# Retention and an exact-GELU MLP on one core: another hand-planned order of groups, with ten chunks turned on TensorE and later places for v and the DMA turns

## The chip, the cores and the metric

The kernel runs on one core of a Trainium2 chip. The metric is the device time of one execution in microseconds. Eight runs of the kernel before have a median of 293.14 us (291.69 to 297.92).

## The reference

Batch 8, 8 heads, sequence 576, head dimension 64; the MLP takes 4608 tokens of width 512 through a hidden width of 2048.

```python
scores = scale * np.matmul(q, k.transpose(0, 1, 3, 2))
gamma = 1.0 - 2.0 ** (-5.0 - np.arange(H))
Dmat = np.where(rel >= 0, gamma[:, None, None] ** rel, 0.0)   # rel = row - column
ret = np.matmul(scores * Dmat, v)
x = ret.transpose(0, 2, 1, 3).reshape(B * S, H * D)
h = x @ w_in
out = (0.5 * h * (1.0 + erf(h / sqrt(2)))) @ w_out
```

All inputs and the output are float32; the kernel computes in bfloat16 with float32 accumulation.

## The kernel before

The sequence of each batch is cut into five chunks, four of 128 tokens and a short one of 64, so that there are 40 chunks. Within a chunk, attention is done with a masked product of scores; what came before a chunk enters through a running state. For a chunk the kernel does these steps:

- load q, k and v, cast to bfloat16, by three to five DMAs of POOL's queue (`load_chunk`, L232 and L236). Nine sets of buffers hold loaded chunks. The loads of w_in (L247, eight pieces) and w_out (L255, eight pieces) stand in the same queue, in the order that the string LOADS writes out ("i", "o" and chunk numbers);
- `turn`: transpose q and k into qkT. The first N_PE_TR chunks are turned on TensorE (L326, L328) and copied out of PSUM by DVE or ACT (L331, L334); the others are turned by a DMA that SP issues (L315). SP also issues the stores of the output (L662, L664);
- `scaled_v`: multiply v by its decay into vh, on DVE (L412);
- `together`: the scores of new chunks, and the products of the state with q of chunks pending (L362); `masked`: the causal mask, on DVE straight from PSUM or by an ACT copy first (L401, L403), as ACT_MASK and the planned load of both engines decide;
- `inner` (o_ps, L438) and `states` (u_ps, L460), whose sum run_sum DVE keeps (L469, L472, L478) and ACT copies out (L475);
- `evacuate`: DVE multiplies o_ps by its decay into xT (L490).

These come in groups: an entry of PLAN says how many new chunks a group takes (0, 1 or 2), how much MLP work is to lie before it, and whether the products ahead of the next group are cut into halves of 64 rows of output. The chunks taken by the last group are the pending ones of the next.

The MLP works on blocks of 512 tokens. The first product makes hT (L303) which ACT turns into g by a GELU (L532). The first N_DYN blocks may take their tokens in pieces, as they come ready. The second product, called fast, multiplies quarter matrices with seven products in place of eight; it needs sums of g, called s, made by DVE (L562 to L565), and sums of w_out, called w_sum (L546 to L549). From block 7 on (N_LEAN) the first product is done so too (lean).

The order is written by a planner that runs while the program is built. It holds a clock, the busy times of DVE and ACT, the eight PSUM banks and a model of the transfers, and at each step emits what is due: a group, a turn, a scaling of v, sums, or else a step of the MLP. Each engine then runs its own instructions in just this order, waiting where the real data is late. A scaling of v is offered when the model says that v has landed, and a turn by DMA when k has; a group when the masks, states, turns and banks that it needs are ready by the model. In the model a load takes LD_FIX + transfer + LD_TAIL, and a DMA turn T_FIX + T_DMA + T_TAIL:

```python
def load(took, at, key, issue=0.87):
    pool_at[0] = max(pool_at[0], clock[0]) + issue
    transfer(0, pool_at[0] - issue + LD_FIX, took, LD_TAIL, at, key)
...
i = nxt["V"]
if i < nxt["T"] and i < nxt["S"] + 5:
    got.append((land_v[i], "V", i))
```

Of the kernel before, what the change touches and what calls it, by code (L numbers as in the profile page):

```python
# [16 lines left out]
def kernel(  # L17
# [24 lines left out]
    C = 128  # L42
# [4 lines left out]
    NCH = -(-S // C)  # L47
    chunks = [(b, ci, ci * C, min(C, S - ci * C)) for b in range(B) for ci in range(NCH)]
    N_CH = len(chunks)
    N_PE_TR = 9  # L50
    N_FIRST = 4
    N_LD = 9
    N_RING = 4
    LD_FIX = 2.5
    LD_TAIL = 1.9
    T_FIX = 2.4
    T_TAIL = 4.2
    T_DMA = 1.8
    N_DYN = 2
    N_LEAN = 7  # L60
    LEAN_FIRST = 1
    LOADS = "1 2 3 i i i 4 5 6 i i i 7 i i 8 o o o o o o o o"
    T_LEAD = 5
    TR_LEAD = 5
    POOL_0 = 1.05
    LAND_0 = (2.9, 4.0, 3.9)
    COLS = ()
    CLOCK_0 = 3.2
    ACT_MASK = 0.3
    X_FROM = 10  # L70
    PLAN = [(1, 207, 1), (1, 571, 0), (0, 547, 0), (2, 777, 0), (1, 404, 0), (2, 522, 0), (1, 106, 0), (1, 13, 1), (2, 31, 0), (1, 74, 0), (0, 58, 0), (1, 9, 0), (2, 46, 0), (1, 68, 0), (2, 53, 0), (2, 58, 0), (2, 6, 0), (2, 102, 0), (2, 3, 1), (2, 116, 0), (2, 78, 0), (2, 78, 0), (2, 34, 0), (0, 6, 0), (2, 51, 1), (2, 51, 0), (2, 35, 1), (0, 0, 1)]
    FAST_FROM = 0
    HALF = TOK_BLK // 2
    COL = d_model // 2
# [23 lines left out]
    clock = [0.0]  # L98
# [12 lines left out]
    def on_dve(ready, n, rate=1):  # L111
        return on("DVE", ready, n / rate / 960 + 0.072)
# [17 lines left out]
    turned = const_pool.tile([128, 32], FP32, name="turned")  # L130
# [44 lines left out]
    land_in, land_out = [1e6] * (N_DF // 2), [None] * (N_DF // 2)  # L175
    w_sum = const_pool.tile([128, 4, N_DF // 2, COL], BF16, name="w_sum")
    land_q, land_k, land_v = {}, {}, {}
    rings = ([], [])
    dma_at = [0.0]
    pool_at = [POOL_0]  # L180
# [22 lines left out]
    def transfer(ring, start, took, tail, at, key):  # L203
# [4 lines left out]
        ahead = tuple([list(job) for job in q_] for q_ in rings)  # L208
        serve(ahead, dma_at[0], 1e5, True)

    def load(took, at, key, issue=0.87):
        pool_at[0] = max(pool_at[0], clock[0]) + issue
        transfer(0, pool_at[0] - issue + LD_FIX, took, LD_TAIL, at, key)

    def head_of(i, place):
# [3 lines left out]
    def load_chunk(i, now=0.0):  # L219
        b, ci, c0, cs = chunks[i]  # L220
        if i == 0:
            loaded[i] = (qk0, v0)
            transfer(1, LAND_0[1] - 3.0, 1.1, 1.0, land_k, i)
            transfer(0, LAND_0[2] - 1.7, 0.87, 0.9, land_v, i)
            land_q[i], land_k[i], land_v[i] = on_dve(LAND_0[0], 512, 1.5), on_dve(LAND_0[1], 512, 1.5), LAND_0[2]
            return
        qk = ld_pool.tile([128, 2, H, D], BF16, tag="qk", name="qk_ld")
        v_ld = ld_pool.tile([128, H, D], BF16, tag="v", name="v_ld")
        for dst, src, at_ in ((qk[:, 0], q, land_q), (qk[:, 1], k, land_k), (v_ld, v, land_v)):
            if i >= X_FROM and src is not v:  # L230
                for odd in range(2):
                    nc.gpsimd.dma_start(dst[:cs, HP * odd:HP * odd + HP],  # L232
                                        src[b, odd::2, c0:c0 + cs, :].rearrange("h s d -> s h d"))
                    load(0.435 * cs / C, at_, i, 0.73)
                continue
            nc.gpsimd.dma_start(dst[:cs], src[b, :, c0:c0 + cs, :].rearrange("h s d -> s h d"))  # L236
            load(0.87 * cs / C, at_, i)
        loaded[i] = (qk, v_ld)

    W_IN_COLS = 256  # L240
# [3 lines left out]
    def load_w_in():  # L244
        j = len(w_in_sb)
        t = const_pool.tile([128, N_DM, W_IN_COLS], BF16, name=f"w_in{j}")
        nc.gpsimd.dma_start(  # L247
            t, moe_w_in[:, j * W_IN_COLS:(j + 1) * W_IN_COLS].rearrange("(c p) f -> p c f", p=128)
        )
        w_in_sb.append(t)  # L250
        load(1.34, land_in, j)

    def load_w_out():
        j = next(j for j in range(N_DF) if land_out[j] is None)
        nc.gpsimd.dma_start(  # L255
            w_out_sb[:, j], moe_w_out[j * 256:(j + 1) * 256, :].rearrange("(c p) f -> p c f", p=128)
        )
        load(1.34, land_out, j)

    load_chunk(0)  # L260
    for what in LOADS.split():
        if what == "i":
# [6 lines left out]
    st = {i: {} for i in range(N_CH)}  # L269
# [35 lines left out]
    def turn(i, parts=(0, 1)):  # L305
# [7 lines left out]
        qkT = s["qkT"]  # L313
        if i >= N_PE_TR:
            nc.sync.dma_start(qkT.rearrange("p j hp s -> p (j hp) s")[:, :, :cs],  # L315
                              qk[:cs].rearrange("p j h d -> p (j h d)"), transpose=True)
            transfer(1, clock[0] + T_FIX, T_DMA * cs / C, T_TAIL, s, "turned")
            return
# [73 lines left out]
    def masked(i):  # L392
# [3 lines left out]
        for e in range(2):  # L396
            r = ret_short[e] if cs < C else ret_pool.tile([128, HP, 128], BF16, tag=f"ret{e}", name=f"ret{e}")
            on_both = max(busy["ACT"], ready) + 0.6 <= max(busy["DVE"], ready) + ACT_MASK
            src, begin = sc[e][:cs, :, :cs], ready
# [428 lines left out]
    stages = []  # L828
    first_runs = [[[("d", t, m)] for m in range(N_DF)] for t in range(N_DYN)]
    second_run = [[("s", t, n) for n in range(len(FAST_ORDER))] for t in range(N_BLK)]  # L830
    stages = [first_runs[0], first_runs[1] + [second_run[0]], [second_run[0]] + first_runs[1], [second_run[1]] + (first_runs[2] if N_DYN > 2 else [])]
    for t in range(2, N_BLK):
        if t < N_LEAN:
            stages.append([[("1", t, m, 0, TOK_BLK) for m in range(N_DF)]] if t >= N_DYN else first_runs[t])
        lean_runs = [[("f", t + 1, n, x) for x in range(len(FIRST_ORDER))] for n in range(N_DF // 4)]
# [49 lines left out]
    def state_to(pend, new):  # L885
        return max([-1] + pend[-1:] + ([new[-1] - 1] if new else []))
# [10 lines left out]
    def group_ready(pend, new):  # L897
        when = max([0.0] + [max(st[i]["masked"], st[i].get("scaled", 1e6)) for i in pend])
        for i in pend:
            if chunks[i][1] > 0:  # L900
                when = max(when, st[i].get("u_end", 0.0) - 0.5)
        when = max([when] + [st[i].get("turned", 1e6) - 0.3 * len(pend) for i in new])
        n = 2 if pend else 0
        for i in range(nxt["U"], state_to(pend, new) + 1):
            if chunks[i][1] + 1 < NCH:
                when = max(when, st[i].get("scaled", 1e6))
                n = 3 if pend else 1
        if n:
            when = max(when, banks_at(n))
        if new:  # L910
            when = max(when, banks_at(n + 2 * len(new)) - 0.3 * n)
        return when

    def attention_picks():
        got = []
        pend, i = held(), nxt["R"]
        pick = mlp_pick()
        kind, t = pick[1][0][:2] if pick is not None else ("s", N_BLK)
        starved = pick is None or pick[0] > clock[0] + 0.3

        if nxt["P"] < len(PLAN):
            size, due, _ = PLAN[nxt["P"]]
            new = list(range(i, i + size))
            if (paced[0] >= due or starved) and i + size <= nxt["T"]:
                got.append((group_ready(pend, new), "G", (pend, new)))
        i = nxt["V"]
        if i < nxt["T"] and i < nxt["S"] + 5:
            got.append((land_v[i], "V", i))
        i = nxt["T"]
        if i < N_CH and i in land_v and i <= nxt["S"] + (T_LEAD if i < N_PE_TR else TR_LEAD):  # L930
            if i >= N_PE_TR:
                got.append((land_k[i], "T", i))
            elif i >= N_FIRST:
                got.append((max(land_k[i] + 0.1, banks_at(2)), "T", i))
            else:
                got.append((max((land_q, land_k)[half[0]][i] + 0.1, banks_at(1)), "T", i))
        if to_sum and fast_done.get(to_sum[0][0] - 1, 0) >= 12:
            got.append((g_ready(to_sum[0][0], 0, TOK_BLK, range(4 * to_sum[0][1], 4 * to_sum[0][1] + 4)) - 0.1, "Z", 0))
        if gelus:
            got.append((gelus[0][0] - 0.1, "H", 0))  # L940
        j = len(w_in_sums)
        if N_LEAN < N_BLK and j < len(w_in_sb) and N_CH - 1 in loaded and nxt["S"] > N_CH - N_LD + j and nxt["U"] > N_CH - N_LD + j:
            got.append((busy["DVE"] + 0.1, "Y", j))
        t = N_LEAN + len(x_sums)
        if t < N_BLK and nxt["V"] == N_CH and x_ready(t * TOK_BLK, (t + 1) * TOK_BLK) < 1e5:
            got.append((max(busy["DVE"] + 0.1, x_ready(t * TOK_BLK, (t + 1) * TOK_BLK)), "X", t))
        if weights_due:
            got.append((weights_due[0][0], "W", 0))
        return got
# [6 lines left out]
    def attend(kind, i):  # L956
        if kind == "G":
            pend, new = i
            nxt["P"] += 1
            p = nxt["P"]  # L960
            by_col[0] = p < len(PLAN) and PLAN[p][2] > 0
            upto = state_to(pend, new)
# [130 lines left out]
```

## Time and profile before

| | |
|---|---|
| median of 8 runs | 293.14 us |
| profiled execution | 293.15 us, span 291.4 us |
| PE busy | 278.7 us (96%) |
| DVE busy | 210.9 us (72%) |
| ACT busy | 155.4 us (53%) |
| POOL busy | 147.4 us (51%), nearly all before 190 us |
| first hT product | 17.34 us |
| last matmul ends | 287.88 us |

A line of the profile names engine, line, operation, and output and inputs by the program's names. "Busy" of PE counts a matmul from start to modelled end; they are pipelined, so start to start is the measure of rate. [...] Line numbers are those of the kernel before; in the changed one, everything behind the model of loads stands up to nine lines further down.

### The profile page before, as it was taken

Reading aid. Unit: us, or ns where it says so; the run is one execution under the profiler, and the core shown is the slowest. Engines: PE = TensorE matmul, PEld = TensorE weight load, DVE = VectorE, ACT = ScalarE, POOL = GpSimd, SP = SyncE. Lnnn points to the kernel's source line nnn. Section 1 sums busy time; section 2 is a strip of 40 time slices with the busy share of each in tenths; the row PEclk is TensorE's granted clock in tenths of the full one; section 3 lists DMA queues with packets and bytes.
Section 4 is the critical chain, followed back from the end, with each engine's and each line's share of the span. In section 5 each row is a group of like instructions: output and inputs, shape, how many; then the busy total and the mean of one; then the engine's idle time right before and its main releaser. Section 6 shows DMA issues by size and latency. Waiting matters only on the chain.

```text
span 291.4 us, 8239 instructions
## 1 busy us (share of the span) xinstructions
PE 278.7 (96%) x3396; PEld 203.2 (70%) x3410; DVE 210.9 (72%) x530; ACT 155.4 (53%) x318; POOL 147.4 (51%) x198
## 2 busy tenths in 40 slices
PE   6799999999999699999999999989999999999995
PEld 2477565988864288557874687548854888888884
DVE  7679982769866974798388747799667885985552
ACT  3766667232356443675167724764257487587221
POOL 8998757997775996884995499200000000000000
PEclk9999999999999799999999999999999999999999
DMA  9999999999999999999999999970030000210123
GB/s 136 156 168 176 177 206 146 141 180 208 154 197 166 137 156 139 166 192 128 147 155 185 136 147 174 133 113 2 2 145 0 2 0 3 107 39 0 75 108 108
DMA packets 154565, 35.79 MB, mean 123 GB/s; under 512 B 143264, under 2 KB 150432, under 8 KB 154528
## 3 DMA queue, kind: packets, MB, share of 16 engines
q0 software_dynamic: 117792, 18.10, 94.8%
q1 hardware_dynamic: 36736, 17.18, 34.1%
q8 instruction: 26, 0.43, 0.7%
q14 instruction: 11, 0.09, 0.1%
HBM read 36.70 MB, written 9.44 MB: 158 GB/s over the span
## 4 chain that ended last, share of the span: by engine, by line
PE 46%; DMA 23%; POOL 16%; DVE 8%; issue 5%; ACT 0%; POOLq 0%; ACTq 0%; DVEq 0%
PE fast L303 24%; DMA v_ld<-in_v_dram 14%; PE hT L303 13%; POOL qk_ld L232 7%; PE lean L303 7%; DMA w_in<-in_moe_w_in_dram 5%; DMA w_out<-in_moe_w_out_dram 3%; POOL v_ld L236 3%; POOL qk_ld L236 3%; POOL w_in L247 1%; DVE s L563 1%; DVE s L562 1%; DVE s L565 1%; PE o_ps L438 1%; DVE ret L403 1%
## 5 line engine op out<-in xcount | busy, mean ns | idle before, releaser
L303 PE MATMUL hT<-xT,w_in 128*128 128x512 bf16 (+7 forms) x639 | 102.6, 341 | 3.8 <-DVE run_sum L472 3.0
L303 PEld LDWEIGHTS <-w_in 128*128 128x128 bf16 (+1 forms) x748 | 59.4, 101 | 50.8 <-DVE run_sum L472 4.0
L532 ACT ACTIVATE g<-hT 128x512 bf16<-128x512 f32 (+5 forms) x143 | 68.8, 507 | 32.5 <-PE hT L303 32.0
L303 PEld LDWEIGHTS <-s 128*128 128x128 bf16 x576 | 56.1, 98 | 6.9 <-DVE s L563 0.2
L232 POOL DMA_DIRECT2D qk_ld<-in_k_dram x60 | 44.1, 752 | 17.5 <-DMA v_ld<-in_v_dram 12.8
L303 PE MATMUL fast<-w_sum,s 128*128 128x256 bf16 x432 | 50.0, 273 | 0.0
L232 POOL DMA_DIRECT2D qk_ld<-in_q_dram x60 | 44.7, 766 | 6.8 <-PE hT L303 4.3
L303 PEld LDWEIGHTS <-g 128*128 128x128 bf16 (+1 forms) x456 | 41.8, 99 | 5.9 <-DVE u_sb L478 0.4
L236 POOL DMA_DIRECT2D v_ld<-in_v_dram x39 | 34.3, 879 | 7.9 <-DVE xT L490 2.8
L303 PE MATMUL fast<-w_out,g 128*128 128x256 bf16 (+1 forms) x312 | 33.8, 273 | 0.0
L654 DVE TENSOR_TENSOR o_sb<-fast,u 128x512 f32<-128x512 f32 (+1 forms) x20 | 12.7, 633 | 26.8 <-ACT u L650 16.2
L650 ACT COPY u<-fast 128x512 f32<-128x512 f32 (+1 forms) x20 | 10.9, 543 | 36.0 <-PE fast L303 36.0
L412 DVE TENSOR_TENSOR vh<-v_ld,dv 128x512 bf16<-128x512 bf16 x32 | 21.5, 680 | 7.5 <-DMA v_ld<-in_v_dram 7.5
L490 DVE TENSOR_TENSOR xT<-o_ps,dq 128x256 bf16<-128x256 f32 (+1 forms) x84 | 26.6, 374 | 0.0
L403 DVE TENSOR_TENSOR ret<-sc,msk 128x512 bf16<-128x512 f32 x29 | 19.1, 683 | 3.5 <-PE o_ps L362 2.8
L475 ACT CAST u_sb<-run_sum 128x256 bf16<-128x256 f32 x24 | 9.7, 405 | 20.5 <-DVE run_sum L469 11.0
L562 DVE TENSOR_TENSOR s<-g 128x512 bf16<-128x512 bf16 x36 | 15.0, 417 | 6.7 <-ACT g L532 6.2
L401 ACT CAST ret<-sc 128x512 bf16<-128x512 f32 x35 | 19.0, 585 | 0.4 <-PE o_ps L362 0.4
L303 PE MATMUL fast<-w_sum,g 128*128 128x256 bf16 x144 | 17.2, 273 | 0.0
L303 PE MATMUL fast<-w_out,s 128*128 128x256 bf16 x144 | 17.2, 272 | 0.0
L563 DVE TENSOR_TENSOR s<-s,g 128x512 bf16<-128x512 bf16 x36 | 15.3, 425 | 1.2
L362 PE MATMUL sc<-qkT 64*64 64x128 bf16 (+1 forms) x576 | 15.7, 220 | 0.1
(89 smaller groups left out, 338.1 us busy)
## 6 DMA issues: line engine op xcount, KB each, us to landing
out_dram<-o_sb SPq DMA_DIRECT2D x16, 512.0 KB, 6.0
v_ld<-in_v_dram POOLq DMA_DIRECT2D x32, 128.0 KB, 6.0
qk_ld<-in_q_dram POOLq DMA_DIRECT2D x50, 64.0 KB, 6.2
qk_ld<-in_k_dram POOLq DMA_DIRECT2D x50, 64.0 KB, 5.5
w_in<-in_moe_w_in_dram POOLq DMA_DIRECT2D x8, 256.0 KB, 6.8
w_out<-in_moe_w_out_dram POOLq DMA_DIRECT2D x8, 256.0 KB, 8.7
out_dram<-o_sb SPq DMA_DIRECT2D x8, 128.0 KB, 1.7
qk_ld<-in_q_dram POOLq DMA_DIRECT2D x7, 128.0 KB, 6.9
```

The costliest lines, as they stand in the source:

```text
L232: nc.gpsimd.dma_start(dst[:cs, HP * odd:HP * odd + HP], src[b, odd::2, c0:c0 + cs, :].rearrange("h s d -> s h d"))
L236: nc.gpsimd.dma_start(dst[:cs], src[b, :, c0:c0 + cs, :].rearrange("h s d -> s h d"))
L303: nc.tensor.matmul(out_[sl], lhsT=lhsT[:, sl], rhs=rhs, start=start, stop=stop, skip_group_check=True)
L362: nc.tensor.matmul(out_, lhsT=lhsT, rhs=rhs, start=start, stop=stop, skip_group_check=True)
L401: nc.scalar.copy(r[:cs, :, :cs], src)
L403: nc.vector.tensor_tensor(r[:cs, :, :cs], src, msk[:cs, :, :cs].to_broadcast([cs, HP, cs]), op=ALU.mult)
L412: nc.vector.tensor_tensor(vh[:cs], loaded[i][1][:cs], dv[:cs, :, ci:ci + 1].to_broadcast([cs, H, D]), op=ALU.mult)
L490: nc.vector.tensor_tensor(xT[:, g::2, at:at + hi - lo], s["o_ps"][g][:, s["place"], :, lo:hi], dq[:, g::2, c0 + lo:c0 + hi], op=ALU.mult)
L532: nc.scalar.activation(g_of(t, m, lo, hi), hT[:, :hi - lo], AF.Gelu)
L562: nc.vector.tensor_tensor(u[:, 0], a[2, 1], a[2, 2], op=ALU.add)
L563: nc.vector.tensor_tensor(u[:, 1], u[:, 0], a[1, 1], op=ALU.subtract)
L654: nc.vector.tensor_tensor(dst, psum(where), f[to][:, sl], op=ALU.add)
```

## The change

It gives the planner other constants and another PLAN, of 34 entries in place of 28. The model of loads lets a load begin only when the eighth load before it has landed. Chunk 9, a short one, is turned on TensorE too. For the chunks turned by DMA, the scaling of v is offered V_SAFE = 3 us after v has landed in the model, and a group that takes the chunk as new G_SAFE = 1.5 us after its turn. N_DYN goes from 2 to 4, and the mask takes the way over ACT less readily. The loads of w_in stand earlier among the chunks. No instruction's kind changes and nothing is added to the loop over chunks; what moves is the order on each engine, and how many pieces the MLP products are cut into.

```diff
-    N_PE_TR = 9
+    N_PE_TR = 10
...
-    LD_FIX = 2.5
-    LD_TAIL = 1.9
-    T_FIX = 2.4
-    T_TAIL = 4.2
-    T_DMA = 1.8
-    N_DYN = 2
+    LD_FIX = 2.0
+    LD_TAIL = 1.7
+    T_FIX = 2.1
+    T_TAIL = 2.6
+    T_DMA = 1.95
+    N_DYN = 4
...
-    LOADS = "1 2 3 i i i 4 5 6 i i i 7 i i 8 o o o o o o o o"
+    LOADS = "1 2 3 i i i i 4 5 i 6 i i 7 i 8 o o o o o o o o"
     T_LEAD = 5
-    TR_LEAD = 5
+    V_SAFE = 3
+    G_SAFE = 1.5
+    TR_LEAD = 6
...
-    ACT_MASK = 0.3
+    ACT_MASK = -0.5
...
-    PLAN = [(1, 207, 1), (1, 571, 0), (0, 547, 0), (2, 777, 0), (1, 404, 0), (2, 522, 0), (1, 106, 0), (1, 13, 1), (2, 31, 0), (1, 74, 0), (0, 58, 0), (1, 9, 0), (2, 46, 0), (1, 68, 0), (2, 53, 0), (2, 58, 0), (2, 6, 0), (2, 102, 0), (2, 3, 1), (2, 116, 0), (2, 78, 0), (2, 78, 0), (2, 34, 0), (0, 6, 0), (2, 51, 1), (2, 51, 0), (2, 35, 1), (0, 0, 1)]
+    PLAN = [(1, 220, 1), (1, 524, 0), (1, 208, 0), (1, 297, 1), (0, 273, 0), (1, 263, 0), (2, 34, 0), (0, 57, 0), (1, 1, 1), (1, 4, 1), (1, 8, 0), (1, 43, 0), (2, 31, 0), (2, 53, 0), (2, 75, 0), (1, 21, 0), (2, 58, 0), (0, 102, 0), (2, 38, 0), (0, 7, 1), (1, 75, 0), (0, 13, 0), (1, 46, 0), (0, 46, 0), (1, 25, 0), (2, 0, 0), (2, 122, 0), (2, 115, 0), (2, 92, 0), (2, 21, 0), (2, 65, 0), (2, 31, 1), (1, 78, 1), (0, 205, 1)]
...
     def load(took, at, key, issue=0.87):
-        pool_at[0] = max(pool_at[0], clock[0]) + issue
+        t = max(pool_at[0], clock[0])
+        if len(in_ring) >= 8:
+            a, k = in_ring[-8]
+            t = max(t, a[k])
+        in_ring.append((at, key))
+        pool_at[0] = t + issue
...
-        when = max([when] + [st[i].get("turned", 1e6) - 0.3 * len(pend) for i in new])
+        when = max([when] + [st[i].get("turned", 1e6) + (G_SAFE if i >= N_PE_TR else 0) - 0.3 * len(pend) for i in new])
...
-            got.append((land_v[i], "V", i))
+            got.append((land_v[i] + (V_SAFE if i >= N_PE_TR else 0), "V", i))
```

The model's transfer of a chunk's q, k or v goes from 0.87 to 0.93 (0.435 to 0.475 for the halves), of a piece of a weight from 1.34 to 1.25.

## The prediction

> **What bounds the kernel now.** I read the page first (engine shares, granted clock), then the waits by engine, then the timelines of DVE and PE around the long ones, then a table of windows, and last the instruction order of both versions.
>
> ```profile
> PE 278.7 (96%) x3396; PEld 203.2 (70%) x3410; DVE 210.9 (72%) x530; ACT 155.4 (53%) x318; POOL 147.4 (51%) x198
> ...
> PEclk9999999999999799999999999999999999999999
> ```
> TensorE is busy 96% of the span: it is the bound, and what moves the end is work added to it or idle time taken from it. One slice (the 14th) has a lower granted clock.
>
> ```profile
> DVE vh_short L412 <- DMA v_ld<-in_v_dram: 8.0, 3, 5.8
> DVE vh L412 <- DMA v_ld<-in_v_dram: 7.5, 7, 1.8
> ...
> PE hT L303 <- DVE run_sum L472: 3.0, 2, 2.2
> ```
> DVE stands 15.5 us in ten waits for a load of v. TensorE has two waits behind DVE's run_sum, 2.18 and 0.84 us. The timeline of DVE shows that they are one story:
>
> ```profile
> 94.40 0.68 DVE L412 TENSOR_TENSOR vh_short<-v_ld,dv 64x512 bf16<-64x512 bf16 x1 [1.66 <-DMA v_ld<-in_v_dram]
> ...
> 96.47 0.41 DVE L469 COPY run_sum<-u_ps 128x256 f32<-128x256 f32 x1
> 97.41 0.42 DVE L472 TENSOR_TENSOR run_sum<-run_sum,u_ps 128x256 f32<-128x256 f32 x1 [0.52 <-ACT u_sb L475]
> ```
> and the timeline of PE, where it ends:
> ```profile
> 97.88 2.61 PE L303 MATMUL hT<-xT,w_in 128*128 128x512 bf16 x8 [2.18 <-DVE run_sum L472]
> ```
> The columns are start, length, engine, line, operation, and in brackets the idle time before it. DVE runs in program order. Scaling the v of a short chunk (chunk 19) waits for its load until 94.40; behind it stand four sums of g and the run_sum copies, which alone free the PSUM bank of u_ps. The next hT has no bank until 97.8. At 188.34 the same happens with the v of chunk 38 (DVE waits 1.78, hT begins at 193.29 after 0.84).
>
> ```profile
> 95.70:98.00 2.30, 0.12 (x1) 0.11 (x2) 1.78 (x6) 0.54 (x2) 2.30 (x4) 1.00 2.56 141
> 98.00:104.00 6.00, 6.00 (x25) 2.73 (x24) 4.52 (x12) 4.02 (x8) 5.80 (x9) 0.72 1.96 134
> 192.00:194.00 2.00, 1.16 (x14) 0.40 (x10) 1.47 (x4) 1.13 (x3) 0.00 (x0) 1.00 0.73 134
> ```
> Columns: window, its length, busy of PE, PEld, DVE, ACT, POOL, then granted clock, DMA share, GB/s. After the 2.18 us of idleness the clock averages 0.72 for 6 us: 6 x 0.28 = 1.7 us lost on top. After 0.84 us it stays at 1.00. Apart from these, the first 17.34 us (until the first hT) and one gap of 0.32 at 256.7 before a lean product, PE has no idle stretch worth naming.
>
> **The change part by part.**
>
> Matmul work. From the two instruction orders: the hT products count 572 in full-width equivalents before (two 64-row halves are one) and 676 after, over the same columns; N_DYN = 4 cuts more blocks into pieces. 64 products of 64 columns took 1.87 us in the trace, 29.2 ns each against 26.7 for 64 columns[...], so 2.5 ns each: 104 x 2.5 = +0.3 us. More of fast and hT is cut into 64-row halves, which cost nothing: 24 halves of 512 columns (34.25 to 36.86) are 2.61 us, 0.2175 a pair, against 0.217 a whole. Chunk 9, a short one, is turned on TensorE: eight transposes, +0.33 (20.07 to 20.40). The attention stretches of PE go from 26 to 29. A stretch with one each of states, inner, scores, cross is 0.93 (75.94 to 76.87), one with two, two, two and one is 1.51 (176.37 on); so one state, inner and score are 0.58, a cross about 0.1, and 0.2 to 0.25 is fixed: +0.6. Sum: +1.2 us, all on the path.
>
> Start. Chunk 0 is now masked wholly by DVE (two of 0.65 from 8.42, done 9.7; before, the second half waited for ACT until 11.2). But the qkT copies of chunk 1 still come off ACT from 10.2 to 11.3, so its scores begin about 11.4 (11.8 before). Then DVE has two vh (1.3 us) ahead of the inner products of chunk 1 (14.7 instead of 13.6 to 14.2), and ret of chunk 2 (1.25) ahead of xT of chunk 1, which so ends about 17.7 instead of 15.9. First hT: about 18.1 instead of 17.34, with 0.4 us more of attention done: +0.4. Bounds: 0 and +0.9.
>
> Load order. The fourth w_in moves ahead of chunk 4, the seventh ahead of chunk 7. A w_in lands every 1.3 us in the trace, a q, k or v every 0.87 to 0.9. By these steps k of chunk 4 lands at 20.7, of 5 at 23.7, of 6 at 27.8 (19.4, 22.4 and 24.8 before); PE reaches their transposes at about 22.6, 24.9 and 28.4. The last weights and chunk 8 land as before (bytes and issues are equal: 194 loads). Taken as 0; bounds 0 and +0.7 (k of chunk 6 at 27.8 is 0.6 ahead of its use).
>
> Masks and gelus. 14 full and 4 short masks lose their ACT copy (14 x 0.585 + 4 x 0.37 = -9.7 us on ACT) and read PSUM on DVE (0.65 instead of 0.37 step: +4 us on DVE); 26 more gelus, each 0.11 beyond its columns, give ACT +3. Both lie beside PE, which covers them: 0, except in the stretch of the first rival below.
>
> v later in DVE's order. I placed each vh between the run_sum before and after it, with the PE work done until then and the trace's landings. Chunk 19 was ahead of the stretch at 93.5 and landed at 94.4; now it is ahead of the one at about 101. Chunks 20 to 37 all come 1 us or more behind their landing, or have over 4 us until the next run_sum. Chunk 39 (landing 192.6) stands ahead of the stretch at about 193.5. So the first wait goes (2.18 and its 1.7 of clock) and the second (0.84): -4.7. What is late next: PE itself, then the last loads.
>
> The clock term needs a choice. Row: 2.18 us idle, then 6 us at 0.72. The Trainium skill ("TensorE: Matmul & The Clock Gate", [...]"HAM oscillation") has a free-running window of about 3.4 us and asks for no idle gaps above it; by that rule a 2.18 us gap is free and the change gains only 3.0. I take the row: the measured half-clock stretch begins 1 us after the gap. By the rule the sum below would be 1.7 worse (292.5).
>
> DMA turns. 31 become 30. Scores of the turned chunks come later on PE: chunk 37 was used at 191.1 with its turn landing at 191.0; now its stretch is some 7 us of PE work later. On SP the turns stand behind stores: that of chunk 36 behind the fourth block's first store, of 37 behind its second, as late as about 174 and 178, with 7 us to land (their median) or the 9 that chunk 36 took: still 4 us ahead of use. Chunk 38 comes nearest: turn landing 193.8, PE there about 193.2. Expected +0.4; bounds 0 and +2.5. POOL's own queue is not reordered after the weights; it is busy 24 us of every 30 until 185, so the loads end at about 192 whatever PE does.
>
> DVE after 50 us. xT of chunk 8, then eight w_sum (0.65 each, 5.2 us), begin about 52.9 and end 58.1; the first product that reads w_sum is due at 58.6. Then two adds, ret of chunk 10, xT, a vh and sixteen sums of g (6.1 us) end about 72.6, due about 72.0 on. Expected +0.3; bounds 0 and +4 (with the clock).
>
> **Sum.** -4.7 + 1.2 + 0.4 + 0.4 + 0.3 = -2.4 us against the profiled execution's 293.15 (span 291.4 and 1.75 around it), which is the median of the runs (293.14): 290.8 us.
>
> **The rivals.**
>
> 1. Slower: the backlog of DVE between 52 and 73 us. For it: DVE takes over 4 us of masks from ACT, w_sum begins 3.1 us later than before (52.9 against 49.8) although fast products start only 1.9 later, and sixteen sums stand in a row right before the product that needs them. Against: margins come out at +0.5 and -0.6, not at several us. If DVE is 1.6 us later than my sum, PE idles 2.2 and the clock halves, 1.7 more: 290.8 + 3.9 = 294.7. Below 1.2 us of backlog it stays a small wait. Chance 0.24.
>
> 2. No change: the gain is given back at the end of the loads. PE comes to chunks 37 to 39 sooner, while POOL and DMA still deliver the last k at 191.6 and v at 192.6. If the turn of 38 lands 1.5 later than in the trace, PE waits about 2: 292.5. For it: 24 of 30 us of POOL busy. Against: the stretches stand a chunk later in the order. The clock falling after smaller gaps than 2.18 would end here too. Chance 0.24.
>
> 3. The sum holds, or the small waits are nil (289.9): 0.52.
>
> **How the numbers follow.** Measurements of this kernel tell about 0.5% (1.5 us) from no change: faster is below 291.7, slower above 294.6. Chances are those of the three cases. The range: from 288.3 (no start cost, no small waits, no price for stretches and cuts: -4.7 + 0.3 = -4.4, and the scatter of the runs, whose lowest was 1.4 under the median, in part) to 296.0 (the first rival and a second wait of 1.3).
>
> **What would show it.** Right: no wait of PE behind run_sum near 95 and 193, PEclk 9 in every slice but the last, DVE's waits for v_ld under 5 us, first hT near 18. Wrong: a wait of fast behind DVE s or w_sum at 58 or 72, PE behind a DMA (qkT or qk_ld) at 193, or a slice of PEclk below 9 elsewhere. If PE's idle time after the first hT is under 1.5 us and the time is still above 292, my price of the added work is what failed.

## The result, and the profile after

The changed kernel takes 289.52 us (median of 21 runs, 288.71 to 292.42), the kernel before 293.18 us (median of 58 runs, 290.28 to 297.92). The ratio is 0.9901, with a 95% interval of 0.9881 to 0.992: 1.0% faster, 3.7 us by the medians. Every ratio here leaves out runs more than 1.5% above their kernel's fastest, so it need not be the ratio of the medians beside it. In the experiments a ratio is always to the kernel before, run beside them (64 runs more, medians 293.64, 293.97 and 294.16 in three batches). The profiled execution took 289.58 us, with a span of 287.8. Predicted were 290.8.

The page after, engine shares and granted clock:

```profile
PE 277.9 (97%) x3666; PEld 212.7 (74%) x3679; DVE 215.2 (75%) x534; ACT 150.5 (52%) x324; POOL 147.3 (51%) x198
...
PEclk9599999999999999999999999999999999999999
```

270 more matmul records, many of them narrow, and yet no more busy time on TensorE. The low digit of the clock in the 14th slice (95 to 102 us) has gone; another stands in the second slice, at the start. The first line of the chain that ended last read "PE 46%; DMA 23%; POOL 16%; DVE 8%; issue 5%" at its head before; now TensorE's own work is nine tenths of it:

```profile
PE 90%; DVE 6%; ACT 2%; issue 1%
```

DVE's waits for v_ld, 15.5 us in ten pieces before, do not occur any more in its list of waits. The timeline of DVE where chunk 19's short v is now scaled (start, length, engine, line, operation; an idle time would follow in brackets):

```profile
97.46 0.68 DVE L421 TENSOR_TENSOR vh<-v_ld,dv 128x512 bf16<-128x512 bf16 x1
...
100.99 0.68 DVE L421 TENSOR_TENSOR vh_short<-v_ld,dv 64x512 bf16<-64x512 bf16 x1
...
103.84 0.42 DVE L573 TENSOR_TENSOR s<-g 128x512 bf16<-128x512 bf16 x1
104.18 0.42 DVE L574 TENSOR_TENSOR s<-g,s 128x512 bf16<-128x512 bf16 x1
104.52 0.41 DVE L481 TENSOR_TENSOR run_sum<-run_sum,u_ps 128x256 f32<-128x256 f32 x1
```

vh_short starts at 100.99 without a wait. The sums s that stand between it and run_sum matter below: a product that reads one of them (103.50 to 103.92) waits 0.22. This and one other are all the waits over 0.1 us that TensorE has after the first hT, as its timeline shows:

```profile
18.36 1.81 PE L312 MATMUL hT<-xT,w_in 128*128 128x256 bf16 x15
...
103.98 0.72 PE L312 MATMUL fast<-w_sum,s 128*128 128x256 bf16 x5 [0.22 <-DVE s L572]
...
126.80 1.47 PE L312 MATMUL hT<-xT,w_in 128*128 128x512 bf16 x5 [0.50 <-issue]
```

**One account for all versions.** In each trace, the end of the last matmul is the start of the first hT, plus TensorE's idle time after it (gaps above 60 ns), plus what was lost to a halved clock (half the length of such stretches), plus work. The work is what remains (before, the last matmul's modelled end is 287.85; the 287.88 given above is the start of the o_sb behind it), in us:

| version | first hT | idle after it | lost to the clock | work | last matmul ends | DVE waits for v_ld |
|---|---|---|---|---|---|---|
| before | 17.34 | 3.68 | 1.7 | 265.1 | 287.85 | 15.5 |
| after | 18.36 | 0.82 | 0 | 265.5 | 284.70 | 0.0 |

Idle time gives 2.9, the clock 1.7; work takes back 0.4 and the start 1.0. That is -3.2, and the tail behind the last matmul is 0.4 shorter: -3.6, the difference of the spans.

### The profile page after: what moved, and what is told of

Read it like the earlier page. It is cut to its first block, busy times and chain, and to the rows that moved or that the text cites. A ratio compares the mean times of both kernels' runs of the same rounds, so it can differ in the third digit from the quotient of the medians.

```text
span 287.8 us, 8792 instructions
## 1 busy us (share of the span) xinstructions
PE 277.9 (97%) x3666; PEld 212.7 (74%) x3679; DVE 215.2 (75%) x534; ACT 150.5 (52%) x324; POOL 147.3 (51%) x198
## 4 chain that ended last, share of the span: by engine, by line
PE 90%; DVE 6%; ACT 2%; issue 1%
PE fast L312 37%; PE hT L312 33%; PE lean L312 9%; PE sc L371 4%; PE o_ps L447 3%; PE u_ps L469 2%; PE o_ps L371 2%; DVE ret L412 1%; PE qk_ps L337 1%; ACT dq L166 1%; DVE xT L499 1%; DVE s L572 1%; DVE s L571 0%; DVE row L127 0%; ACT L169 0%
## 5 line engine op out<-in xcount | busy, mean ns | idle before, releaser
L312 PE MATMUL hT<-xT,w_in 128*64 128x512 bf16 (+9 forms) x797 | 101.7, 315 | 1.2 <-issue 0.5
L312 PEld LDWEIGHTS <-w_in 128*128 128x128 bf16 (+1 forms) x904 | 67.0, 101 | 39.7 <-issue 0.9
L541 ACT ACTIVATE g<-hT 128x512 bf16<-128x512 f32 (+7 forms) x169 | 72.5, 454 | 32.9 <-PE hT L312 31.1
L312 PEld LDWEIGHTS <-s 128*128 128x128 bf16 (+1 forms) x640 | 56.8, 100 | 6.5 <-DVE s L572 0.5
L312 PE MATMUL fast<-w_sum,s 128*128 128x256 bf16 (+1 forms) x480 | 49.3, 273 | 0.2 <-DVE s L572 0.2
L499 DVE TENSOR_TENSOR xT<-o_ps,dq 128x256 bf16<-128x256 f32 (+1 forms) x84 | 26.8, 373 | 4.9 <-PE o_ps L371 4.9
L412 DVE TENSOR_TENSOR ret<-sc,msk 128x512 bf16<-128x512 f32 x43 | 27.6, 682 | 1.9 <-PE sc L371 1.2
L571 DVE TENSOR_TENSOR s<-g 128x512 bf16<-128x512 bf16 x36 | 15.0, 416 | 4.8 <-ACT g L541 4.4
L312 PE MATMUL fast<-w_sum,g 128*128 128x256 bf16 (+1 forms) x160 | 17.2, 273 | 0.0
L312 PE MATMUL fast<-w_out,s 128*128 128x256 bf16 (+1 forms) x160 | 17.2, 272 | 0.0
L573 DVE TENSOR_TENSOR s<-g 128x512 bf16<-128x512 bf16 x36 | 15.0, 417 | 0.0
```

The costliest lines, as they stand in the source:

```text
L312: nc.tensor.matmul(out_[sl], lhsT=lhsT[:, sl], rhs=rhs, start=start, stop=stop, skip_group_check=True)
L412: nc.vector.tensor_tensor(r[:cs, :, :cs], src, msk[:cs, :, :cs].to_broadcast([cs, HP, cs]), op=ALU.mult)
L499: nc.vector.tensor_tensor(xT[:, g::2, at:at + hi - lo], s["o_ps"][g][:, s["place"], :, lo:hi], dq[:, g::2, c0 + lo:c0 + hi], op=ALU.mult)
L541: nc.scalar.activation(g_of(t, m, lo, hi), hT[:, :hi - lo], AF.Gelu)
L571: nc.vector.tensor_tensor(u[:, 0], a[2, 1], a[2, 2], op=ALU.add)
L573: nc.vector.tensor_tensor(u[:, 2], a[1, 1], a[2, 1], op=ALU.subtract)
```

## The experiments

The theory: a scaled v that waits for its load, in DVE's queue ahead of run_sum, is what held TensorE; moving v behind other DVE work is the gain. The rivals: the new list of groups alone does it; the safety margins do it; or the gain belongs to no single part. None of the eleven median times lies in the range that its theory gave, so what follows is read from where the waits went, and the times are given beside it.

### v later, by the planner's account only

In the kernel before, one chunk's v is offered 3 us later, and then every later chunk's:

```diff
-            got.append((land_v[i], "V", i))
+            got.append((land_v[i] + (3 if i == 19 else 0), "V", i))         # first
+            got.append((land_v[i] + (3 if i >= N_PE_TR else 0), "V", i))    # second
```

First:

> The kernel before, with the scaling of v of chunk 19 alone offered 3 us later. Theory (v ahead of run_sum blocks DVE, and the gap on TensorE lowers the clock): the wait at 95 us goes with its 1.7 us of half clock, the one at 193 stays: 289.3 us. If the gap counts without the clock: 291.0. Rival (the gain of the change is the list of groups, not v): 293.2.

Second:

> The kernel before, with v of every chunk turned by DMA offered 3 us later, its list of groups and model of transfers as they were. Theory: both waits of TensorE behind run_sum go, and none of the change's added work (1.2) or later start (0.4) is paid: 288.5 us, less than the changed kernel. Rival (list of groups): 293.2, or slower, as the old groups are not made for late v.

Measured: 293.29 us, ratio 0.9941 (0.99 to 0.9981), and 292.87 us, 0.9949 (0.9895 to 1.0003). DVE still waits for v_ld, 17.5 and 12.8 us. The timelines of the first, DVE then PE, show why:

```profile
94.91 0.69 DVE L412 TENSOR_TENSOR vh<-v_ld,dv 128x512 bf16<-128x512 bf16 x1 [2.40 <-DMA v_ld<-in_v_dram]
```

```profile
98.41 3.63 PE L303 MATMUL hT<-xT,w_in 128*128 128x512 bf16 x16 [1.19 <-DVE run_sum L472]
```

With chunk 19's v pushed back, chunk 20's takes the same place and waits 2.40, and hT waits 1.19 behind run_sum instead of 2.18. What is late next was the next v. The planner packs whatever it believes ready into DVE's queue, so a later offer moves the wait but doesn't end it. Idle time after the first hT is 4.88 and 4.39, above the 3.68 of before. The ratios say half a per cent faster, the second with an interval that reaches 1; by the medians of all runs (293.64 before) it is 0.1 and 0.3%. So a gain is not shown, and the times of 289.3 and 288.5 that were expected did not come.

### v later in DVE's queue, and nothing else

So v was moved in the program itself: the planner's accounts stay, and the instructions of all other engines keep their order. Each vh of a chunk from N_PE_TR on is written behind the next group's run_sum, masks and xT, unless that group reads it.

```diff
     def scaled_v(i):
+        st[i]["scaled"] = on_dve(land_v[i], 512) + BACK
+        if i >= N_PE_TR:
+            late_v.append(i)
+        else:
+            write_v(i)
...
             upto = state_to(pend, new)
+            while late_v and late_v[0] <= max([upto] + pend):
+                write_v(late_v.pop(0))
...
             nxt["R"] += len(new)
+            while late_v:
+                write_v(late_v.pop(0))
```

> The kernel before with the order of TensorE, ACT, SP and POOL kept instruction for instruction; on DVE alone each vh of a chunk turned by DMA is written behind the next group's run_sum, masks and xT (ahead of it where that group reads it). Theory (a vh at the head of DVE's queue blocks run_sum, and TensorE behind it): DVE's waits for v_ld fall from 15.5 to under 6 us, TensorE's idle time after the first hT from 3.7 to under 1.5: 288.5 to 290 us. Rival (the old groups use their chunks too early, so that the wait only moves, as when v alone was offered later): 292 to 293.5.

Measured: 291.46 us, ratio 0.9946 (0.9907 to 0.9984). DVE's waits for v_ld fall from 15.5 to 0.5 us. DVE, then PE, at the place of the old wait:

```profile
95.10 0.42 DVE L573 TENSOR_TENSOR s<-g,s 128x512 bf16<-128x512 bf16 x1
96.30 0.43 DVE L477 COPY run_sum<-u_ps 128x256 f32<-128x256 f32 x1 [0.78 <-PE u_ps L468]
```

```profile
96.98 3.19 PE L303 MATMUL hT<-xT,w_in 128*128 128x512 bf16 x13
```

run_sum now waits 0.78 for TensorE's u_ps, not TensorE for run_sum, and hT goes through. This shows that the scaling of v in DVE's queue made both of the waits behind run_sum. It also shows that their end alone is not the whole gain: a new wait stands at 68.72, where three vh lie ahead of an o_sb that frees the bank of hT,

```profile
PE hT L303 <- DVE o_sb L662: 1.1, 1, 1.1
```

and with remainders of 0.2 to 0.4 the idle time is 3.41. Of 3.0 us removed, 2.75 came back elsewhere; what the profile gains is the half clock (1.7 to 0), which the section on the prediction comes back to. How much of the change's gain v's place is worth is less sure than the mechanism: about half by the ratios (0.54% against 0.99%, the first with an interval of 0.16 to 0.93%) and by the profiled spans (1.7 of 3.6 us), but 0.9% by the medians of all runs made side by side (291.46 against 294.16).

### The margin ahead of v

```diff
-    V_SAFE = 3
+    V_SAFE = 0
```

> The changed kernel with V_SAFE = 0. Theory: DVE waits for v_ld again (over 5 us in all) and TensorE behind it at one place or two: 291.5 to 293.5 us. Rival (the groups lie a chunk later and the model of loads is right, so v's place does not matter): 289.5, no TensorE wait over 0.5.

Measured, in the changed kernel: 290.69 us, ratio 0.9879 (0.9824 to 0.9933), not to be told from the change. DVE waits 3.2 us for v_ld again, in two places (2.17 at 63.42, 1.06 at 165.94), and idle time is 1.46 instead of 0.82, but no wait of TensorE follows one of these. In the new order the margin is not what keeps v off TensorE's path.

### The list alone, and everything but the list

> The kernel before with the new list of groups alone: old model of transfers, v offered when the model has it. Theory: DVE waits for v as before, TensorE stalls behind it: 292 to 294 us. Rival (the list of groups carries the gain): 289.5 to 290.5.

> The changed kernel with the old list of groups (new model of loads, V_SAFE and G_SAFE kept). After the first four runs the theory is another: neither v's place nor the list carries the gain alone, but a plan made with loads that land when they do on the chip. Theory now: few waits of TensorE after the first hT (under 1.5 us in all), time set by the work and the start: 289.5 to 291.5 us. Rival (the new list is needed as well, as the old one brings groups at the old places): TensorE waits of 2 us or more again, 292 to 295.

The first is the kernel before with the new PLAN, the second the changed kernel with the old one:

```diff
-    PLAN = [(1, 207, 1), (1, 571, 0), (0, 547, 0), ...
+    PLAN = [(1, 220, 1), (1, 524, 0), (1, 208, 0), ...
```

Measured: 299.5 us, ratio 1.022 (1.016 to 1.0281), and 298.21 us, 1.0105 (1.004 to 1.0169). Either half by itself is slower than the kernel before. With the new list alone DVE waits less for v than before (8.5 us), yet one of these waits passes to TensorE, and with a larger gap than before; DVE, then PE:

```profile
169.79 0.69 DVE L412 TENSOR_TENSOR vh<-v_ld,dv 128x512 bf16<-128x512 bf16 x1 [2.93 <-DMA v_ld<-in_v_dram]
```

```profile
176.22 2.10 PE L303 MATMUL fast<-w_out,g 128*128 128x256 bf16 x9 [3.11 <-DVE run_sum L472]
```

Between them DVE works off twelve sums and the first part of run_sum without a pause; the second part, at 175.74, waits 0.53 for ACT. The other large gap, 2.93 at 88.40, has no wait for v in it: hT stands there behind xT, and DVE is busy all the time. Idle time is 8.48 in all.

With the old list and the rest of the change, DVE waits for no v at all (0.0), and yet idle time is 7.40. The list of PE's waits has it:

```profile
PE o_ps L447 <- DVE ret L412: 4.5, 2, 4.2
```

o_ps stands behind two ret, and they behind eight sums, two copies, a vh and a run_sum, all of which DVE works off without a pause. So an absent wait for v is not enough: the order must also put what TensorE needs next ahead of what it needs later.

### One constant at a time, or all of the transfer model

In the changed kernel, first all constants of transfers as they were (the diff shows four of them) and no limit of eight open loads; then only that limit taken out; then only the margin of the turns taken out:

```diff
-    LD_FIX = 2.0
-    LD_TAIL = 1.7
-    T_FIX = 2.1
-    T_TAIL = 2.6
+    LD_FIX = 2.5
+    LD_TAIL = 1.9
+    T_FIX = 2.4
+    T_TAIL = 4.2
...
-        if len(in_ring) >= 8:
-            a, k = in_ring[-8]
-            t = max(t, a[k])
...
-    G_SAFE = 1.5
+    G_SAFE = 0
```

> The changed kernel with the old model of loads and turns (old constants, no limit of eight open loads), the new list, V_SAFE and G_SAFE kept. Theory (the model's fit carries it): v, k and turns are used before they land, TensorE waits of 2 us or more, half clock behind them: 292 to 296 us. Rival (the two safety margins are enough): 289.5 to 290.5.

> The changed kernel without the limit of eight open loads in the model, its new constants kept. Theory: loads of the model run ahead of the chip by what POOL waits for open loads, groups come too early: 291.5 to 295 us. Rival (constants and margins are enough): 289.5 to 290.5.

> The changed kernel with G_SAFE = 0: groups may take a chunk 1.5 us sooner after its DMA turn. Theory (loads fit, the turns had 4 us in hand): 289.5 to 290.3 us, no TensorE wait for qkT. Rival (the margin of the turns carries part of the gain): scores wait for qkT, 291 to 293.

| | us | ratio | idle after first hT | largest gap, at |
|---|---|---|---|---|
| old constants | 297.89 | 1.0101 (1.0033 to 1.0169) | 7.43 | 3.24 at 106.86 |
| no limit of open loads | 296.77 | 1.0106 (1.0065 to 1.0147) | 6.57 | 3.08 at 106.67 |
| no margin for turns | 295.41 | 1.0055 (1.0014 to 1.0096) | 4.79 | 3.08 at 106.31 |

Three different edits make one gap at one place. None of them waits there for a load or a turn, as the theories of the first two had it (without the margin for turns, too, TensorE waits for no turn): the gap is fast behind a sum s. The timeline of DVE with the old constants:

```profile
101.01 0.41 DVE L478 TENSOR_TENSOR run_sum<-run_sum,u_ps 128x256 f32<-128x256 f32 x1
101.34 1.28 DVE L409 TENSOR_TENSOR ret<-sc,msk 128x512 bf16<-128x512 f32 x2
102.54 1.41 DVE L496 TENSOR_TENSOR xT<-o_ps,dq 128x256 bf16<-128x256 f32 x4
103.87 0.68 DVE L418 TENSOR_TENSOR vh<-v_ld,dv 128x512 bf16<-128x512 bf16 x1
...
106.38 0.42 DVE L569 TENSOR_TENSOR s<-s,g 128x512 bf16<-128x512 bf16 x1
```

and PE, which reads that s:

```profile
106.86 1.38 PE L309 MATMUL fast<-w_sum,s 128*128 128x256 bf16 x11 [3.24 <-DVE s L569]
```

In the changed kernel the last eight sums (101.59 to 104.18) stand ahead of run_sum (104.52, shown above); here the group stands ahead of the sums, and its ret and xT put them some 3 us later. DVE is not idle for a moment. The list of groups was made for one set of constants; under another the same list yields another order, and this one place turns over. So these three do not price the limit or the margin by itself: they price a flipped order.

### How late may run_sum be

The changed kernel with seven copies that nobody needs (zeros from a part of dq, 4.76 us in all) ahead of chunk 27's run_sum, near 151 us. The order on every engine stays.

```diff
+                if j == 27:
+                    for _ in range(7):
+                        nc.vector.tensor_copy(zeros, dq[:, 0, :512])
```

> The changed kernel with seven casts (0.6 us each) on DVE ahead of one run_sum near 150 us, written into a tile that is not read again; all other orders are kept. Theory (banks leave about 1 us of slack): TensorE idles 2 to 3 us once, 291.5 to 292.5 us, and in part of the executions, by chance of the clock's window, half clock adds 1.7 to 3.4. Rival (slack of several us hides it): 289.5 to 290.

Measured: 295.71 us, ratio 1.0108 (1.0041 to 1.0174). The two parts of run_sum on DVE, in the changed kernel without the copies and here with them, then PE:

```profile
149.79 0.42 DVE L481 TENSOR_TENSOR run_sum<-run_sum,u_ps 128x256 f32<-128x256 f32 x1 [1.57 <-PE u_ps L469]
150.74 0.42 DVE L481 TENSOR_TENSOR run_sum<-run_sum,u_ps 128x256 f32<-128x256 f32 x1 [0.53 <-ACT u_sb L484]
```

```profile
151.08 0.42 DVE L484 TENSOR_TENSOR run_sum<-run_sum,u_ps 128x256 f32<-128x256 f32 x1 [1.57 <-PE u_ps L469]
151.42 4.76 DVE L479 CAST zeros<-dq 128x512 bf16<-128x512 f32 x7
156.09 0.41 DVE L484 TENSOR_TENSOR run_sum<-run_sum,u_ps 128x256 f32<-128x256 f32 x1
```

```profile
156.56 1.68 PE L312 MATMUL hT<-xT,w_in 128*128 128x512 bf16 x7 [3.42 <-DVE run_sum L484]
```

Without the copies the second part of run_sum starts 0.95 us after the first, waiting 0.53 for ACT; with them 5.01. So it is 4.06 us later, not 4.76, since the copies use up that wait, and TensorE idles 3.42. The slack of this place is about 0.6 us, and nearly the whole delay passes to TensorE. One delay was tried at one place; the slack at 95 us in the kernel before was not measured. The median is 6.2 us above the changed kernel's 289.52, more than the gap: in the profiled execution, the lowest of the six, the last matmul ends 4.9 us later (289.59), of which 1.15 is a longer wait at 128.09, ahead of the copies. The rest of the 6.2 us is not explained.

### The start

The changed kernel begins its first hT 1.0 later than before. Here the two copies of chunk 1's qkT go to DVE, and the memsets of the short buffers move behind chunk 3's masks:

```diff
-                nc.scalar.copy(qkT[:, j, :, :cs], ps_[:, :, :cs])
+                (nc.vector.tensor_copy if i == 1 else nc.scalar.copy)(qkT[:, j, :, :cs], ps_[:, :, :cs])
...
             if new[:1] == [0]:
                 for t in ret_short + [vh_short]:
-                    nc.vector.memset(t, 0.0)
```

> The changed kernel with its start eased: the two qkT copies of chunk 1 go from ACT to DVE and three memsets of 0.8 us in all move behind the masks of chunk 3; TensorE's order is kept. Theory (TensorE's wait of 1.0 us for qkT at 11.3 is on the path of the first hT): first hT 0.7 us sooner, 288.8 us. Rival (DVE's chain of masks sets the first hT): 289.5 or a little more.

Measured: 290.26 us, ratio 0.9926 (0.9889 to 0.9964), no better than the change (0.9901). PE:

```profile
17.04 1.92 PE L312 MATMUL hT<-xT,w_in 128*128 128x256 bf16 x16
...
27.16 2.12 PE L312 MATMUL hT<-xT,w_in 128*128 128x512 bf16 x11 [0.59 <-DMA w_in<-in_moe_w_in_dram]
```

The first hT comes 1.3 sooner than in the changed kernel's profile (18.36), but part of that is the clock. The kernel without the margin for turns has the same start, instruction for instruction, and its first hT stands at 17.83: there the clock rises for good at 10.31 and here at 9.28, in the changed kernel's profile at 14.5. So the edit itself gives about 0.8, as expected. TensorE then waits for w_in further on (0.59 here, 0.18 at 19.14), and idle time is 2.04 instead of 0.82: of the 1.2 us given back, 0.8 goes to loads of w_in and 0.25 to the sum at 104 us.

## Why the prediction was right, and where its sizes were off

**Stalls, -4.7.** Held in the profiled executions: with the small waits of the last two terms, -4.0 was forecast and -4.6 measured (idle 3.68 to 0.82, clock 1.7 to 0). The two waits behind run_sum are gone, and moving v alone shows that v's place in DVE's queue made them. What the step missed is that their end is not yet a gain: moved alone, 2.75 of 3.0 us came back. That nothing came in their place here goes with the whole list and its constants together; this is inferred from the halves being slower, and no run shows which part does it.

**The clock, 1.7 of these.** The Trainium skill ("TensorE: Matmul & The Clock Gate", "HAM oscillation") would have given a gap of 2.18 us no price, and its row here did. The row was right for this execution, but the gap's length is not the reason: in the experiments, gaps of 2.93 and 3.11 us left the clock at half, gaps of 3.24 and 3.42 at full, and of two of 3.08 one each. What decides is how a gap lies to steps of 3.413 us. In each of the thirteen traces the granted clock changes only at whole multiples of 3.413 us from its first change: in the profile of before it rises at 10.18, falls at 98.93 and rises at 102.34, which is 26 and 1 steps. Taking these steps as windows, here is the kernel before (window, its length, busy of PE, PEld, DVE, ACT, POOL, then the granted clock):

```profile
95.51:98.92 3.41, 1.23 (x6) 0.51 (x6) 2.89 (x7) 1.46 (x4) 3.21 (x5) 1.00 2.53 142
98.93:102.34 3.41, 3.41 (x9) 1.18 (x8) 3.38 (x10) 2.00 (x5) 3.41 (x6) 0.50 1.93 118
```

and the kernel with the old constants:

```profile
101.60:105.01 3.41, 1.96 (x16) 1.27 (x14) 3.38 (x9) 1.46 (x4) 3.41 (x6) 1.00 2.13 182
105.02:108.43 3.41, 1.57 (x15) 1.41 (x16) 3.38 (x9) 0.00 (x0) 3.41 (x6) 1.00 2.01 179
108.44:111.84 3.40, 3.40 (x34) 3.04 (x32) 0.23 (x1) 0.99 (x2) 2.84 (x5) 1.00 2.46 139
```

The 2.18 us lie within one window, and the clock is at half in the next. The 3.24 us fall across two, and it stays at full. All the large gaps, with TensorE's idle time in each window that they touch:

| version | gap | idle in its windows | clock behind |
|---|---|---|---|
| before | 2.18 | 2.18 | half |
| new list alone | 2.93 | 1.31, 2.06 | half |
| new list alone | 3.11 | 2.03, 1.08 | half |
| no margin for turns | 3.08 | 2.65, 0.43 | half |
| old list, rest of the change | 4.17 | 0.51, 3.41, 0.57 | half |
| no limit of open loads | 3.08 | 1.87, 1.21 | full |
| old constants | 3.24 | 1.46, 1.85 | full |
| old constants | 2.02 | 1.82 in the larger | full |
| seven copies | 3.42 | 1.68, 1.79 | full |

Some of these windows hold a smaller gap too. In all thirteen traces, of some 1000 windows behind the first hT that begin at full clock, the five with 2.03 us or more of idle time are followed by half clock, and none with 1.87 or less is. The halved stretches last one or two windows, 3.4 or 6.8 us. That fits what the same page says under "What's actually happening", that the window of 3413 ns runs free of the program; its rule of idle gaps above 3.4 us does not fit, as 2.03 us within one window were enough here.

So the 1.7 us were not a fixed price: which windows a gap meets differs from one execution to the next, and it was luck that the profiled one had its gap within a single window. By the limits above, a gap of 2.18 us halves the clock in about half of the positions that it can have (an estimate: 2 us or so of it must lie in one window of 3.41). The runs agree in size. Of the kernel before's 45 runs beside the experiments that the ratios count, 19 had a mean granted clock of 0.997 or more, with a median of 292.13 us, and 26 a lower one, with 293.73. Of the changed kernel's 22 runs, the profiled one among them, 17 had 0.997 or more, with a median of 289.46. At full clock the change is thus worth about 2.7 us (these two groups were not run beside each other), more than the 0.7 that the forecast leaves without its 1.7.

**Work, +1.2: the term that was off.** 0.4 was measured on this pair of traces. The account scatters (265.05 to 265.5 in five traces with the old list, 265.5 to 266.7 in eight with the new one, the means 0.8 apart), so the term was 0.4 to 0.8 too high. The price of a cut comes out of the trace: between the 29.2 ns of a product of 64 columns and the 217 of one of 512 lie 26.8 for each 64, which leaves 2.4 for the product itself. Which of the other prices was too high, the stretches of attention or the 64-row halves, is not separated.

**Start, +0.4.** First hT was forecast at 18.1 and came at 18.36, but the two profiles had different clocks. Before, the clock rises for good at 10.18: four transposes take 0.58 us at 8.98 and 0.38 at 12.82 (the views write 1.00 for the time ahead of a trace's first clock record, so the page's digits don't show this). The changed kernel's profile had full clock from 4.3 to 7.7 and half from 7.7 to 14.5; that is the low digit in the second slice, which the prediction listed as a sign against itself, and not a gap. The same start with the clock rising at 10.31 has its first hT at 17.83: on a like clock the price is +0.5, close to the forecast, and the other half of the 1.0 is the clock. The kernels with v later by the planner's account show the same from the other side: with half clock from about 7.5 to 17.7 the first hT stood at 18.55 and 18.52.

**Last loads, +0.4, and DVE, +0.3.** The first did not come: no wait of TensorE on a DMA at 190. The second is the 0.22 at 103.98, not in the stretch from 52 to 73, where the forecast of DVE's times was good: w_sum was to run from 52.9 to 58.1 ahead of a product at 58.6, and ran from 53.2 to 58.3 ahead of one at 58.74.

**The rivals.** The DVE backlog did not occur between 52 and 73, and no slower version came by way of it there. Its kind is real, though: sums behind a group's masks and xT cost 3.1 to 3.2 us at 106 in three kernels, and masks behind sums cost 4.17 at 43 with the old list. In the changed kernel the sums at 104 stand ahead of the group, and the price there is 0.22. The rival of the last loads had no part: DVE's and TensorE's waits for loads there are nil.

**Open.** The rest of the gain, beyond v's place, lies in waits of 0.2 to 1.1 us that the deferred v leaves and the change does not have. Which constant or entry of the list removes them could not be told, since three of the four edits of constants turned the order over. What holds TensorE at 126.80 (0.50, "issue"; 1.65 at 128.09 with the seven copies) has no releaser in the trace.

## What to carry to other kernels

An instruction that waits for a DMA holds all that is behind it on its engine: put it behind the copies and sums that free PSUM banks for TensorE, and look at once for what takes its place, since here 2.75 of 3.0 us came back until the whole order fitted. A list that was searched against a model belongs to that model's constants: either half alone cost 1 to 2%, and one altered constant flipped a place worth 3 us. Price the clock behind a short gap only as a chance, by how much of the gap can fall into one window, and compare two starts only at a like clock.

## What the runs showed of the hardware

- Granted clock: it changed only in steps of 3.413 us. Behind the first hT a step with 2.03 us or more of TensorE idle time was followed by half clock (2.18 us in the kernel before), and one with 1.87 or less was not, so that a gap of 3.42 us across two steps cost nothing in clock.
- The phase of these steps and the clock at the start differ between executions: full clock came for good at 10.18 in the profile of before, and at about 17.7 in two others with its start, moving the first hT from 17.34 to 18.5.
- With v out of the way in DVE's queue, twelve runs lay between 290.28 and 291.82, while the kernel before on the same chip lay between 290.63 and 297.19. Part of that scatter goes with the clock (over the three batches 292.13 at a mean clock of 0.997 or more, 293.73 below it); the rest was not tried further.
